# Band attention and two layers, one core: token tiles reused in place, first forms from sums made on GpSimd

## The chip, the cores and the metric

The program runs on one core of a Trainium2 chip in a single launch; the host only lays the arrays out. The metric is the device time of one execution in microseconds, from the first to the last instruction and what lies around them.

## The reference

Attention over 4 batches, 8 heads, 512 local and 32 global tokens, head dimension 64, and then two feed-forward layers on the 2176 tokens with model width 512 and inner width 2048. All in fp32:

```python
s_g = scale * q_g @ k_all.T ;  out_g = sm(s_g) @ v_all          # 32 global rows, all keys
s_ll = where(|pos_i - pos_j| <= 32, scale * q_l @ k_l.T, -1e9)  # band of the local rows
out_l = sm([scale * q_l @ k_g.T, s_ll]) @ [v_g, v_l]
x = [out_g, out_l], heads side by side                           # (2176, 512)
h = x @ w_in1 ;  x = where(h > 0, h, exp(min(h, 0)) - 1) @ w_out1
h = x @ w_in2 ;  x = where(h >= 1, h, where(h <= -1, 0, (h+1)**2/4)) @ w_out2
```

## The kernel before

**Arithmetic.** Each fp32 operand of a large product is split in two fp32r parts, high and low, and a product takes three matmuls (low by high, high by low, high by high). Weights come from DRAM as fp32 words which `decode` (L194) splits with integer operations on VectorE and copies on ScalarE; for up blocks `decode_in` (L872) also makes sums of blocks on GpSimd.

**Attention (L414 to L830).** 24 units, their instructions in a fixed order on each engine (`Pinned`). Meanwhile `prep` (L186) loads and decodes the weights of the inner blocks f = 0, 1, 2 of the first layer in six pieces through one tile `wraw`, and the first five up products are made. Each batch j leaves its 512 local tokens in `xh[j]`, `xl[j]`, 128x(4x512) in fp32r.

**Plain blocks.** For f = 0, 1, 2 (`PLAIN[0]`) and then f = 3 (`PLAIN[1]`) the first layer is computed directly: `plain` (up, L273), activation, `down` (L360), for each batch j. Down sums of f = 0, 1, 2 are evicted to DRAM (`collect`, L342); those of later blocks are accumulated there (L344). The 128 global tokens go as rows (L285, L373).

**Forms.** From f = 4 on, and in the whole second layer, two inner blocks and two batches (a duo: batches 0 and 1, or 2 and 3) are multiplied with 7 block products in place of 8 (`quad`, L1044). Each takes a form of the tokens (`X11, X21, X22`, which are quarters of the tokens as they are, and `T1` to `T4`, which are differences) of 128x1024 in two parts, 1 MB, and a form of the weights. 14 pairs of blocks, two duos each, make the groups (L1222). Only one duo's forms are in SBUF; the 28 forms lie in DRAM, and as the last product of a group is done with a form, that of the next group is loaded into its slot (`load_form`, L999).

**The first forms.** `keep_tokens` (L919) stores the tokens of each batch to `sums[0, j]`, high parts by SP (L922) and low parts by an accumulating DMA on GpSimd's queue (L923), and the halves that are `X11, X21, X22` as forms (L927). `first_forms` (L938) reads the sums back into one `wraw` tile, one `top` and one `rest` tile, takes four differences on VectorE, and makes T2, T3, T1, T4 one by one: `split` (ScalarE L934, VectorE L845) into a `wraw` tile and a store (L959). There are two `wraw` buffers and one of `top` and of `rest`. `decode_one` (f = 3), `decode_in`, `decode_out` and `first_forms` all pass through these three, and `in_order` (L171) keeps them in the order of the program on their tiles.

**Order.** After the attention a planner arranges instructions on each engine by a simulated timeline, within data dependences. The order of the program comes from `event` (L1170): at each event a product is issued, perhaps one `down`, and a step of the jobs that have come due (`job_at`). Jobs before: `decode_one` at 0, `decode_in(0)` at 2, `first_forms(0)` at 4, `decode_in(1)` at 8, `first_forms(1)` at 10, `decode_out(0)` at 13 and `decode_out(1)` at 14. The forms of the first group are loaded at event 13, after the token tiles have been closed (L1213).

Of the kernel before, what the change touches and what calls it, by code (L numbers as in the profile page):

```python
# [77 lines left out]
def band_attention_then_two_mlps(  # L78
# [32 lines left out]
    w_ctx, x_ctx = ExitStack(), ExitStack()  # L111
    ring_p = w_ctx.enter_context(tc.tile_pool(name="w", bufs=1))
    plain_p = x_ctx.enter_context(tc.tile_pool(name="xp", bufs=1))
    xh, xl = {}, {}
    for j in range(B):
        xh[j], xl[j] = (plain_p.tile([P, KT, SL], F32R, name=f"x{nm}{j}") for nm in "hl")
# [77 lines left out]
    def decode(wtmp_p, raw, hi, lo):  # L194

        n = raw.shape[1]
        words = raw.bitcast(U32).rearrange("p (n two) -> p n two", two=2)
        low, high = words[:, :, 0], words[:, :, 1]
        top = wtmp_p.tile([P, n], U32, tag="top", name="top")
        rest = wtmp_p.tile([P, n], U32, tag="rest", name="rest")  # L200
        yield

        if eng is free:
            in_order("top", eng.scalar.activation(top.bitcast(F32), high.bitcast(F32), AF.Abs))  # L204
        in_order(
            "rest",
            eng.vector.tensor_scalar(
                rest, high, 0x1FF, 15, ALU.bitwise_and, ALU.logical_shift_left
            ),
        )  # L210
# [12 lines left out]
        eng.vector.tensor_scalar(top, top, 3, 0x3FFFF000, ALU.logical_shift_left, ALU.bitwise_and)  # L223
        eng.vector.scalar_tensor_tensor(  # L224
            top, high, 0xC0000000, top, ALU.bitwise_and, ALU.bitwise_or
        )
        yield
        eng.scalar.activation(hi, top.bitcast(F32), AF.Copy)
        power = raw.bitcast(U32)[:, 0:n]
        eng.vector.tensor_scalar(power, top, 0xFF800000, None, ALU.bitwise_and)  # L230
        eng.vector.scalar_tensor_tensor(  # L231
            lo, rest, 2.0 ** -35, power.bitcast(F32), ALU.mult, ALU.mult
        )
# [24 lines left out]
    class Up:  # L258
# [8 lines left out]
        def products(self, m):  # L267
            ws = w_in[self.layer, self.f]
            for k in range(self.k, self.k + m):
                kt = k // 3  # L270
                w, x = ((ws[1], xh), (ws[0], xl), (ws[0], xh))[k % 3]
                w, x = w[:, kt * P:(kt + 1) * P], x[self.j][:, kt, :]
                eng.tensor.matmul(self.ps, w, x, start=k == 0, stop=k == 3 * KT - 1)  # L273
            self.k += m

# [122 lines left out]

    def x_high(j, kts, at, src):

        eng.scalar.activation(xh[j][:, kts[0]:kts[-1] + 1, at], src, AF.Copy)

    def x_low(j, kts, at, src):

        at = (slice(None), slice(kts[0], kts[-1] + 1), at)
        eng.vector.tensor_tensor(xl[j][at], src, xh[j][at].bitcast(F32), ALU.subtract)
# [493 lines left out]
    def decode_out(n):  # L900

        layer, fs = of_pair(n)
        i = (n + 1) % 3
        raw = words(DM, [(w1, w2)[layer][f][:, KT * P:] for f in fs])
        yield

        while w_out_uses.get(n - 3):
            yield
        w = w_ps[i].tile([P, 2, 2, DM], F32R, tag=f"wo{i}", name="wo")
        for _ in decode(wtmp_p, raw, *(w[:, i].rearrange("p f d -> p (f d)") for i in range(2))):  # L910
            pass
        for i, f in enumerate(fs):
            w_out[layer, f] = [w[:, part, i] for part in range(2)]

    def halves_of(t):

        return t.rearrange("p (k n) -> p k n", k=2)

    def keep_tokens():  # L919

        for j in range(B):
            eng.sync.dma_start(sums[0, j], xh[j].bitcast(F32))  # L922
            eng.gpsimd.dma_start(sums[0, j], xl[j].bitcast(F32), accum_op=ALU.add)  # L923
        for duo in range(2):
            for i, j, h in ((X11, 0, 0), (X21, 0, 1), (X22, 1, 1)):
                for part, x in enumerate((xh, xl)):
                    eng.sync.dma_start(  # L927
                        halves_of(forms[0, duo, i][:, part, :]),
                        x[2 * duo + j][:, 2 * h:2 * h + 2, :].bitcast(F32),
                    )  # L930

    def split(out, src):

        ins = eng.scalar.activation(out[:, 0], src, AF.Copy)  # L934
        add(out[:, 1], src, out[:, 0].bitcast(F32), ALU.subtract)
        return ins

    def first_forms(duo):  # L938

        s = wraw_p.tile([P, KT, SL], F32, tag="wraw", name="sum")
        in_order("wraw", eng.sync.dma_start(s, sums[0, 2 * duo]))
        parts = []
        for tag, h in (("top", 0), ("rest", 1)):
            t = wtmp_p.tile([P, 2 * SL], F32, tag=tag, name="half")
            in_order(tag, eng.sync.dma_start(halves_of(t), sums[0, 2 * duo + 1][:, 2 * h:2 * h + 2, :]))
            parts.append(t)
        yield
        x11, x21 = (s[:, 2 * h:2 * h + 2, :].rearrange("p k n -> p (k n)") for h in range(2))  # L950
        x12, x22 = parts
        add(x11, x12, x11, ALU.subtract)
        add(x12, x22, x12, ALU.subtract)
        add(x22, x22, x11, ALU.subtract)
        add(x21, x21, x22, ALU.subtract)
        for i, src in ((T2, x22), (T3, x12), (T1, x11), (T4, x21)):
            t = wraw_p.tile([P, 2, 2 * SL], F32R, tag="wraw", name="form")
            in_order("wraw", split(t, src))
            eng.sync.dma_start(forms[0, duo, i], t.bitcast(F32))  # L959
            made_forms.add((0, duo, i))  # L960
            yield

    def later_forms(duo):

        j0, j1 = 2 * duo, 2 * duo + 1

        def make(i, src):
            slot[i] = xs_p.tile([P, 2, 2 * SL], F32R, tag=f"x{i}", name="xs")
            split(slot[i], src)
            eng.sync.dma_start(forms[1, duo, i], slot[i].bitcast(F32))  # L970
            made_forms.add((1, duo, i))
            holds[i] = 1, duo

        def until(i):
# [23 lines left out]

    def load_form(layer, duo, i):  # L999

        slot[i] = xs_p.tile([P, 2, 2 * SL], F32R, tag=f"x{i}", name="xs")
        eng.sync.dma_start(slot[i].bitcast(F32), forms[layer, duo, i])
        holds[i] = layer, duo


# [17 lines left out]
    def product(n, duo, col, i, then):  # L1023
# [3 lines left out]
        for k in range(2):  # L1027
            for t, (a, b) in enumerate(((1, 0), (0, 1), (0, 0))):
                eng.tensor.matmul(  # L1029
                    ps,  # L1030
                    w[:, a, col + k * P:col + (k + 1) * P],
                    x[:, b, k * SL:(k + 1) * SL],
                    start=k + t == 0,
                    stop=k == 1 and t == 2,
                )
# [134 lines left out]
    def event(fn):  # L1170
# [7 lines left out]
        for job in line[:2]:  # L1178

            if job in line and (job is line[0] or (job[2] and not job[1])):  # L1180
                step(job)
        now[0] += 1

    def job_at(n, job, ahead=True):

        due.setdefault(n, []).append((job, ahead))

    keep_tokens()
# [5 lines left out]
    for duo in range(2):  # L1194
        made_forms.update((0, duo, i) for i in (X11, X21, X22))
    for i, fs in enumerate(PLAIN):
        for j in range(B):
# [5 lines left out]
        for j in range(B):  # L1203
            for f in fs:
                if (0, f, j) not in born:
                    if i:
                        need(lambda: (0, f) in w_in)
                    event(lambda: plain(0, f, j))
        event(begin)
    while downs and downs[0][2 if downs[0][0] == "down" else 4] == PLAIN[0]:  # L1210
        pop()
    need(lambda: all((0, duo, i) in made_forms for duo in range(2) for i in range(7)))
    x_ctx.close()  # L1213
    w_ctx.close()
    w_ps.append(mpool("w_third", 1))
    xs_p = mpool("xs", 1)
    w_ps.append(mpool("w_last", 1))
# [7 lines left out]
    job_at(base, decode_out(0))  # L1225
    for c in range(7):
        at = base + 17 * c
        job_at(at + 1, decode_out(2 * c + 1))
# [99 lines left out]
```

## Time and profile before

| | |
|---|---|
| time, median of 3 runs | 923.75 us (920.61 to 924.33) |
| profiled execution | 921.4 us, its span 919.6 us |
| busy in the span | PE 91%, VectorE 74%, ScalarE 60%, GpSimd 25% |
| mean granted TensorE clock | 0.957 |
| DMA | 196.59 MB, mean 214 GB/s |

PE is TensorE's matmuls, PEld its weight loads, DVE VectorE, ACT ScalarE, POOL GpSimd, SP SyncE; a q behind a name is the engine's queue (waits and DMA issues). `xs<-form` names an output and an input. In the views a wait `A <- B: us, times, longest` is idle time of A that B ended.

### The profile page before, as it was taken

How to read it: one execution, taken by the hardware profiler on the slowest of the kernel's cores; microseconds unless marked ns; L12 is line 12 of the kernel's file. 1: busy time of each engine (PE TensorE's matmuls, PEld its weight loads, DVE VectorE, ACT ScalarE, POOL GpSimd, SP SyncE). 2: the span in 40 equal slices, each digit the busy share in tenths (PEclk: the TensorE clock that was granted, in tenths of full speed). 3: DMA queues.
4: the chain of work that ended last, by engine and by line, in shares of the span. 5: the costliest groups of instructions: out<-in, count | busy, mean ns of one | idle time of the engine just before them, and what ended most of it. 6: DMA issues, size and time to landing. Idle time of an engine off the chain costs nothing.

```text
span 919.6 us, 15850 instructions
## 1 busy us (share of the span) xinstructions
PE 832.7 (91%) x6058; PEld 673.3 (73%) x6058; DVE 684.8 (74%) x1187; ACT 556.0 (60%) x948; POOL 227.3 (25%) x250
## 2 busy tenths in 40 slices
PE   8769779999942699999999998899989999999998
PEld 5647557887721588888888887688778888888886
DVE  5758567745441999998597988979998889876563
ACT  5657566655451556665563645777787677667461
POOL 2121210402240055345141003033053244421000
PEclk9999899999975799999999999899999999999999
DMA  8997995749999474996495294644676197519733
GB/s 263 326 329 264 298 314 190 231 190 361 362 228 299 166 129 113 294 254 126 69 296 185 98 369 174 256 155 140 208 260 145 26 292 256 94 38 283 258 108 103
DMA packets 59788, 196.59 MB, mean 214 GB/s; under 512 B 8513, under 2 KB 8769, under 8 KB 48193
## 3 DMA queue, kind: packets, MB, share of 16 engines
q1 hardware_dynamic: 47328, 170.15, 51.7%
q0 software_dynamic: 12096, 25.17, 16.9%
q8 instruction: 48, 0.79, 0.3%
q10 hardware_dynamic: 288, 0.26, 0.1%
q14 instruction: 28, 0.22, 0.1%
HBM read 123.99 MB, written 71.57 MB: 213 GB/s over the span
## 4 chain that ended last, share of the span: by engine, by line
PE 62%; DVE 14%; DMA 13%; ACT 5%; issue 3%; POOL 2%; SPq 0%; DVEq 0%; ACTq 0%; POOLq 0%
PE dn L360 28%; PE up L1029 21%; DMA wraw<-in_w 7%; DMA form<-form 3%; PE up L273 2%; DMA half<-sum 2%; DVE u L845 2%; DVE rest L211 2%; PE dn L373 2%; PE s L141 2%; POOL mixed L845 1%; DVE top L224 1%; PE up L285 1%; PE up L141 1%; ACT sn L141 1%
## 5 line engine op out<-in xcount | busy, mean ns | idle before, releaser
L1029 PE MATMUL up<-xs,wi 128*128 128x512 f32 x1176 | 296.0, 398 | 23.8 <-DMA xs<-form 17.1
L360 PE MATMUL dn<-gh,wo 128*128 128x512 f32 x928 | 288.0, 396 | 17.1 <-DVE wo L231 11.2
L1029 PEld LDWEIGHTS up<-xs,wi 128*128 128x128 f32 x1176 | 223.8, 192 | 75.8 <-DMA xs<-form 10.6
L360 PEld LDWEIGHTS dn<-gh,wo 128*128 128x128 f32 x928 | 175.1, 191 | 58.0 <-DVE wo L231 12.5
L360 PE MATMUL dn<-gl,wo 128*128 128x512 f32 x464 | 178.2, 394 | 1.4 <-DVE gl L326 1.4
L845 DVE TENSOR_TENSOR u<-up,u 128x512 f32<-128x512 f32 x196 | 130.6, 684 | 42.4 <-PE up L1029 39.3
L344 POOL DMA_DIRECT2D sum<-ev x80 | 73.2, 1144 | 202.5 <-ACT ev L339 201.7
L322 ACT ACTIVATE gh<-g 128x512 fp32r<-128x512 f32 x123 | 77.5, 630 | 72.1 <-DVE g L305 33.6
L326 DVE TENSOR_TENSOR gl<-g,gh 128x512 fp32r<-128x512 f32 x123 | 102.7, 842 | 23.5 <-ACT gh L322 22.4
L360 PEld LDWEIGHTS dn<-gl,wo 128*128 128x128 f32 x464 | 88.3, 190 | 20.5 <-DVE gl L326 1.8
L845 POOL TENSOR_TENSOR whole<-wi 128x1024 f32<-128x1024 f32 x14 | 36.7, 2624 | 259.6 <-DVE wi L231 183.6
L298 ACT ACTIVATE g<-u,half_sb 128x512 f32<-128x512 f32 x64 | 45.8, 720 | 51.6 <-DVE u L845 44.2
L307 DVE TENSOR_TENSOR g<-u,g 128x512 f32<-128x512 f32 x64 | 52.0, 815 | 25.7 <-ACT g L300 25.6
L339 ACT ACTIVATE ev<-dn 128x512 f32<-128x512 f32 x110 | 60.6, 595 | 10.8 <-DMA sum<-ev 5.4
L293 ACT ACTIVATE g<-u 128x512 f32<-128x512 f32 x48 | 30.2, 629 | 52.4 <-DVE u L845 48.5
L305 DVE SCALAR_TENSOR_TENSOR g<-u,g 128x512 f32<-128x512 f32 x48 | 40.3, 842 | 18.7 <-ACT g L295 18.7
L211 DVE SCALAR_TENSOR_TENSOR rest<-wraw,rest 128x1024 uint32<-128x1024 uint32 x29 | 53.2, 1834 | 0.2
L299 ACT ACTIVATE g<-g,one_sb 128x512 f32<-128x512 f32 x68 | 48.6, 719 | 1.3
L295 ACT ACTIVATE g<-g,one_sb 128x512 f32<-128x512 f32 (+1 forms) x64 | 45.7, 716 | 1.6
L204 ACT ACTIVATE top<-wraw 128x1024 f32<-128x1024 f32 x29 | 33.3, 1147 | 19.4 <-DMA wraw<-in_w 15.8
L141 POOL TENSOR_SCALAR k_sb<-k_sb 128x512 f32<-128x512 f32 (+1 forms) x46 | 21.6, 486 | 89.2 <-DMA k_sb<-in_kT 64.0
L300 ACT ACTIVATE g<-g 128x512 f32<-128x512 f32 x68 | 42.3, 626 | 1.2
(172 smaller groups left out, 1197.2 us busy)
## 6 DMA issues: line engine op xcount, KB each, us to landing
xs<-form SPq DMA_DIRECT2D x49, 1024.0 KB, 9.3
wraw<-in_w SPq DMA_DIRECT2D x56, 512.0 KB, 6.5
sum<-ev POOLq DMA_DIRECT2D x80, 256.0 KB, 8.3
v_sb<-in_vwin SPq DMA_DIRECT2D x64, 260.0 KB, 5.3
form<-xs SPq DMA_DIRECT2D x14, 1024.0 KB, 4.1
sum<-ev SPq DMA_DIRECT2D x32, 256.0 KB, 3.1
sum<-sum SPq DMA_DIRECT2D x8, 1024.0 KB, 4.9
form<-form SPq DMA_DIRECT2D x8, 1024.0 KB, 5.6
```

The source lines that it names most:

```text
L141: return lambda *args, **kw: tc.keep_in_program_order(fn(*args, **kw))
L211: eng.vector.scalar_tensor_tensor(rest, low, 17, rest, ALU.logical_shift_right, ALU.bitwise_or)
L298: eng.scalar.activation(self.g, self.ps, AF.Relu, bias=half_sb, scale=-0.5)
L299: eng.scalar.activation(self.g, self.g, AF.Relu, bias=one_sb, scale=-1.0)
L307: eng.vector.tensor_tensor(g, self.ps, g, ALU.max)
L322: eng.scalar.activation(self.gh, self.g, AF.Copy)
L326: eng.vector.tensor_tensor(self.gl, self.g, self.gh.bitcast(F32), ALU.subtract)
L339: eng.scalar.activation(out, ps, AF.Copy)
L344: eng.gpsimd.dma_start(to, out, accum_op=ALU.add)
L360: eng.tensor.matmul(banks[d], w[:, d * P:(d + 1) * P], g, start=first and k == 0, stop=last and k == 2)
L845: return (engine or eng.vector).tensor_tensor(out, a, b, op)
L1029: eng.tensor.matmul(ps, w[:, a, col + k * P:col + (k + 1) * P], x[:, b, k * SL:(k + 1) * SL], start=k + t == 0, stop=k == 1 and t == 2,)
```

## The change

- The token tiles become 16 tiles of 128x(2x512) (a half of the model width, one part, one batch), in a pool that lives to the end. `PLACES` gives each of the 7 forms one of these places; X11, X21 and X22 of the first duo are the tokens where they lie. The eighth place takes every third block of decoded down weights. The pool `xs`, and `w_last`, are gone.
- `keep_tokens` is gone. `first_forms` adds high and low parts on GpSimd, straight from the token tiles, into the tiles that held the sums before. The copies of X11, X21, X22 to DRAM wait for the last low part of the attention (`last_low`) and are issued by `first_forms`; there is no accumulating DMA of tokens.
- Jobs: `first_forms(0)` at 0, `first_forms(1)` at 2, `decode_one` at 4, `decode_in(0)` at 7, `decode_out(0)` at 9, `decode_in(1)` at 11. With more than two jobs in line an event takes two rounds of steps. f = 3 takes the batches in the order 2, 3, 0, 1, and the early weights' memory is given up after its first batch.
- In the attention's `decode` the last step uses a tile `power` of its own instead of writing over `wraw`.

```diff
-    plain_p = x_ctx.enter_context(tc.tile_pool(name="xp", bufs=1))
+    plain_p = ctx.enter_context(tc.tile_pool(name="xp", bufs=1, reuse_waits="tile"))
+    def token_tile(j, h, part):
+        return plain_p.tile([P, 2, SL], F32R, tag=f"x{part}{j}{h}", name="x" + "hl"[part])
...
+        if eng is pinned:
+            power = wtmp_p.tile([P, n], U32, tag="power", name="power")
+        else:
+            power = raw.bitcast(U32)[:, 0:n]
...
-        power = raw.bitcast(U32)[:, 0:n]
         eng.vector.tensor_scalar(power, top, 0xFF800000, None, ALU.bitwise_and)
...
+        last_low[0] = eng.vector.tensor_tensor(out, src, high, ALU.subtract)
...
+        while len(w_ps) < 2:
+            yield
+        if i < 2:
+            w = w_ps[i].tile([P, 2, 2, DM], F32R, tag=f"wo{i}", name="wo")
+            w = [w[:, part] for part in range(2)]
+        else:
+            w = [token_tile(1, 0, part) for part in range(2)]
...
-    def keep_tokens():
-        for j in range(B):
-            eng.sync.dma_start(sums[0, j], xh[j].bitcast(F32))
-            eng.gpsimd.dma_start(sums[0, j], xl[j].bitcast(F32), accum_op=ALU.add)
...
+    PLACES = {X11: (0, 0), X21: (0, 1), X22: (1, 1), T2: (2, 0), T3: (2, 1), T1: (3, 0), T4: (3, 1)}
+    def new_form(i):
+        slot[i] = [flat(token_tile(*PLACES[i], part)) for part in range(2)]
+        return slot[i]
...
+    def keep(form, key, after=None):
+        for part in range(2):
+            ins = eng.sync.dma_start(forms[key][:, part], form[part].bitcast(F32))
+            if after is not None:
+                tc.add_manual_dep(ins.ins, after.ins.name, LANDED, reason="behind the loads")
+        made_forms.add(key)
...
     def first_forms(duo):
-        s = wraw_p.tile([P, KT, SL], F32, tag="wraw", name="sum")
-        in_order("wraw", eng.sync.dma_start(s, sums[0, 2 * duo]))
...
+        s = wraw_p.tile([P, 2, 2 * SL], F32, tag="wraw", name="sum")
+        x11, x21 = s[:, 0], s[:, 1]
+        x12, x22 = (wtmp_p.tile([P, 2 * SL], F32, tag=tag, name="half") for tag in ("top", "rest"))
+        for out, j, h, tag in ((x11, j0, 0, "wraw"), (x12, j1, 0, "top"), (x22, j1, 1, "rest"), (x21, j0, 1, "")):
+            high, low = (flat(x[j][h]).bitcast(F32) for x in (xh, xl))
+            ins = add(out, high, low, engine=eng.gpsimd)
+            if tag:
+                in_order(tag, ins)
+        for i, j, h in ((X11, j0, 0), (X21, j0, 1), (X22, j1, 1)):
+            keep([flat(x[j][h]) for x in (xh, xl)], (0, duo, i), last_low[0])
         yield
         add(x11, x12, x11, ALU.subtract)
         ...
         for i, src in ((T2, x22), (T3, x12), (T1, x11), (T4, x21)):
             t = wraw_p.tile([P, 2, 2 * SL], F32R, tag="wraw", name="form")
+            t = [t[:, part] for part in range(2)]
             in_order("wraw", split(t, src))
-            eng.sync.dma_start(forms[0, duo, i], t.bitcast(F32))
-            yield
+            keep(t, (0, duo, i))
+            if i == T3:
+                yield
...
-    job_at(0, decode_one(PLAIN[1][0]))
-    job_at(2, decode_in(0))
-    job_at(4, first_forms(0), False)
-    job_at(8, decode_in(1))
-    job_at(10, first_forms(1), False)
+    job_at(0, first_forms(0), False)
+    job_at(2, first_forms(1), False)
+    job_at(4, decode_one(PLAIN[1][0]))
+    job_at(7, decode_in(0))
+    job_at(9, decode_out(0))
+    job_at(11, decode_in(1))
+    for i, js in enumerate(((0, 1, 2, 3), (2, 3, 0, 1))):
...
-    for i in range(7):
+    for i, (j, h) in ((X11, (0, 0)), (X21, (0, 1)), (X22, (1, 1))):
+        slot[i] = [flat(x[j][h]) for x in (xh, xl)]
+        holds[i] = 0, 0
...
+    for i in (T2, T3, T1, T4):
         load_form(0, 0, i)
```

## Rows read from the trace of the kernel before

**Rows 1.** The page: busy tenths of TensorE, 40 slices of 23 us

```profile
PE   8769779999942699999999998899989999999998
```

**Rows 2.** Engine times by stage: busy us (instructions), clock, DMA share, GB/s

```profile
0.00:150.00 150.00, 118.52 (x2846) 88.55 (x2850) 96.20 (x441) 93.86 (x244) 30.91 (x85) 0.94 0.88 291
155.30:219.40 64.10, 64.10 (x296) 53.56 (x294) 39.25 (x48) 40.37 (x63) 9.22 (x7) 1.00 0.71 242
219.40:252.00 32.60, 29.23 (x131) 23.45 (x131) 18.27 (x27) 14.94 (x24) 12.70 (x11) 0.95 1.04 381
252.00:312.20 60.20, 21.94 (x60) 14.68 (x58) 27.51 (x31) 21.61 (x31) 9.55 (x11) 0.60 0.88 252
```

**Rows 3.** Waits, 160 to 320 us: us in total, times, longest

```profile
PE up L1029 <- DMA xs<-form: 17.1, 3, 9.8
PE dn L360 <- DVE wo L231: 11.2, 2, 10.3
```

**Rows 4.** The chain that ended last, 150 to 420 us: start, us, what

```profile
206.23 1.24 DVE form L845
...
216.18 1.17 ACT top L204
...
230.75 2.38 POOL wi L845
...
233.15 19.61 DMA half<-sum
...
260.18 6.11 DMA form<-form
...
268.74 10.51 DMA form<-form
...
288.46 1.24 DVE form L845
...
290.56 8.61 DMA wraw<-in_w
...
299.26 0.71 DVE rest L207
...
304.57 1.24 DVE wo L231
```

**Rows 5.** Timeline of SP's queue: first stores of the made forms

```profile
186.58 6.54 SPq L959 DMA_DIRECT2D form<-form  x2
```

**Rows 6.** Instructions of L923: count, ns min/median/max, first and last start

```profile
L923 POOL DMA_DIRECT2D sum<-xl x4: 878/884/1024, 52.2 to 161.8; - x4
```

**Rows 7.** Timeline of VectorE in the attention: two stretches

```profile
26.17 0.43 DVE L141 TENSOR_SCALAR rest<-wraw 128x512 uint32<-128x512 uint32 x1 [2.88 <-DMA wraw<-in_w]
...
87.51 0.69 DVE L141 SCALAR_TENSOR_TENSOR top<-wraw,top 128x512 uint32<-128x512 uint32 x1
...
91.64 0.69 DVE L141 SCALAR_TENSOR_TENSOR wl<-rest,wraw 128x512 fp32r<-128x512 uint32 x1
```

**Rows 8.** Waits of SP's queue, 0 to 150, and of VectorE, 0 to 160

```profile
SPq L141 <- DVE wl L141: 12.7, 4, 4.3
...
DVE rest L141 <- DMA wraw<-in_w: 18.9, 6, 5.4
```

**Rows 9.** Groups of TensorE instructions by line, 155.3 to 330 us

```profile
L360 PE MATMUL dn<-gh,wl 128*128 128x512 f32 x42 | 16.4, 392 | 0.0
L273 PE MATMUL up<-xh,wl 128*128 128x512 f32 x24 | 9.3, 389 | 0.0
```

**Rows 10.** Timeline of all engines, 223.3 to 228.3 us

```profile
223.38 2.40 POOL L845 TENSOR_TENSOR whole<-wi 128x1024 f32<-128x1024 f32 x1 [48.00 <-DVE wi L231]
...
227.04 1.14 DVE L326 TENSOR_TENSOR gl<-g,gh 128x512 fp32r<-128x512 f32 x1 [0.70 <-ACT gh L322]
...
228.10 0.68 DVE L845 TENSOR_TENSOR u<-up,u 128x512 f32<-128x512 f32 x1
```

**Rows 11.** Timeline of ScalarE: first write of the new top tile

```profile
151.04 1.17 ACT L204 ACTIVATE top<-wraw 128x1024 f32<-128x1024 f32 x1 [0.67 <-PE po L141]
```

More of the change, by code (lines that the diff above doesn't have):

```diff
@@ L110, in band_attention_then_two_mlps @@
     ev_p = [ctx.enter_context(tc.tile_pool(name="ev", bufs=2))]
-    w_ctx, x_ctx = ExitStack(), ExitStack()
+    plain_p = ctx.enter_context(tc.tile_pool(name="xp", bufs=1, reuse_waits="tile"))
+    w_ctx = ExitStack()
     ring_p = w_ctx.enter_context(tc.tile_pool(name="w", bufs=1))
-    plain_p = x_ctx.enter_context(tc.tile_pool(name="xp", bufs=1))
+    def token_tile(j, h, part):
+        return plain_p.tile([P, 2, SL], F32R, tag=f"x{part}{j}{h}", name="x" + "hl"[part])
     xh, xl = {}, {}
     for j in range(B):
-        xh[j], xl[j] = (plain_p.tile([P, KT, SL], F32R, name=f"x{nm}{j}") for nm in "hl")
+        for part, x in enumerate((xh, xl)):
+            x[j] = [token_tile(j, h, part) for h in range(2)]
     xh[GR], xl[GR] = (xpool.tile([P, KT, B * SG], F32R, name=f"x{nm}{GR}") for nm in "hl")
@@ L271, in products @@
                 w, x = ((ws[1], xh), (ws[0], xl), (ws[0], xh))[k % 3]
-                w, x = w[:, kt * P:(kt + 1) * P], x[self.j][:, kt, :]
+                w, x = w[:, kt * P:(kt + 1) * P], x[self.j][kt // 2][:, kt % 2, :]
                 eng.tensor.matmul(self.ps, w, x, start=k == 0, stop=k == 3 * KT - 1)
@@ L399, in x_high, with tokens @@
     def x_high(j, kts, at, src):
-        eng.scalar.activation(xh[j][:, kts[0]:kts[-1] + 1, at], src, AF.Copy)
+        eng.scalar.activation(tokens(xh, j, kts, at), src, AF.Copy)
     def x_low(j, kts, at, src):
-        at = (slice(None), slice(kts[0], kts[-1] + 1), at)
-        eng.vector.tensor_tensor(xl[j][at], src, xh[j][at].bitcast(F32), ALU.subtract)
+        out, high = tokens(xl, j, kts, at), tokens(xh, j, kts, at).bitcast(F32)
+        last_low[0] = eng.vector.tensor_tensor(out, src, high, ALU.subtract)
+    def tokens(x, j, kts, at):
+        if j == GR:
+            return x[j][:, kts[0]:kts[-1] + 1, at]
+        return x[j][kts[0] // 2][:, kts[0] % 2:kts[-1] % 2 + 1, at]
+    last_low = [None]
     def mpool(name, bufs, **kw):
@@ L908, in decode_out @@
             yield
-        w = w_ps[i].tile([P, 2, 2, DM], F32R, tag=f"wo{i}", name="wo")
-        for _ in decode(wtmp_p, raw, *(w[:, i].rearrange("p f d -> p (f d)") for i in range(2))):
+        while len(w_ps) < 2:
[5 more added lines that the diff above has]
+            w = [token_tile(1, 0, part) for part in range(2)]
+        for _ in decode(wtmp_p, raw, *(part.rearrange("p f d -> p (f d)") for part in w)):
@@ L911, in decode_out @@
             pass
         for i, f in enumerate(fs):
-            w_out[layer, f] = [w[:, part, i] for part in range(2)]
-    def halves_of(t):
-        return t.rearrange("p (k n) -> p k n", k=2)
-    def keep_tokens():
-        for j in range(B):
-            eng.sync.dma_start(sums[0, j], xh[j].bitcast(F32))
-            eng.gpsimd.dma_start(sums[0, j], xl[j].bitcast(F32), accum_op=ALU.add)
[L924 to L930, printed above, removed]
+            w_out[layer, f] = [part[:, i] for part in w]
@@ L932, in split, with flat @@
+    PLACES = {X11: (0, 0), X21: (0, 1), X22: (1, 1), T2: (2, 0), T3: (2, 1), T1: (3, 0), T4: (3, 1)}
+    def flat(t):
+        return t.rearrange("p k n -> p (k n)")
+    def new_form(i):
+        slot[i] = [flat(token_tile(*PLACES[i], part)) for part in range(2)]
+        return slot[i]
     def split(out, src):
-        ins = eng.scalar.activation(out[:, 0], src, AF.Copy)
-        add(out[:, 1], src, out[:, 0].bitcast(F32), ALU.subtract)
-        return ins
-    def first_forms(duo):
-        s = wraw_p.tile([P, KT, SL], F32, tag="wraw", name="sum")
-        in_order("wraw", eng.sync.dma_start(s, sums[0, 2 * duo]))
[L944 to L948, printed above, removed]
+        ins = eng.scalar.activation(out[0], src, AF.Copy)
+        add(out[1], src, out[0].bitcast(F32), ALU.subtract)
+        return ins
@@ new lines, in keep @@
+    def keep(form, key, after=None):
[4 more added lines that the diff above has]
+        made_forms.add(key)
+    def first_forms(duo):
+        j0, j1 = 2 * duo, 2 * duo + 1
+        s = wraw_p.tile([P, 2, 2 * SL], F32, tag="wraw", name="sum")
[8 more added lines that the diff above has]
+            keep([flat(x[j][h]) for x in (xh, xl)], (0, duo, i), last_low[0])
@@ L949, in first_forms @@
         yield
-        x11, x21 = (s[:, 2 * h:2 * h + 2, :].rearrange("p k n -> p (k n)") for h in range(2))
-        x12, x22 = parts
         add(x11, x12, x11, ALU.subtract)
@@ L957, in first_forms @@
             t = wraw_p.tile([P, 2, 2 * SL], F32R, tag="wraw", name="form")
+            t = [t[:, part] for part in range(2)]
             in_order("wraw", split(t, src))
-            eng.sync.dma_start(forms[0, duo, i], t.bitcast(F32))
-            made_forms.add((0, duo, i))
-            yield
+            keep(t, (0, duo, i))
+            if i == T3:
+                yield
     def later_forms(duo):
@@ L967, in make @@
         def make(i, src):
[L968 to L971, printed above, removed]
+            split(new_form(i), src)
+            keep(slot[i], (1, duo, i))
             holds[i] = 1, duo
@@ L999, in load_form @@
     def load_form(layer, duo, i):
-        slot[i] = xs_p.tile([P, 2, 2 * SL], F32R, tag=f"x{i}", name="xs")
-        eng.sync.dma_start(slot[i].bitcast(F32), forms[layer, duo, i])
+        for part, t in enumerate(new_form(i)):
+            eng.sync.dma_start(t.bitcast(F32), forms[layer, duo, i][:, part])
         holds[i] = layer, duo
@@ L1031, in product @@
                     w[:, a, col + k * P:col + (k + 1) * P],
-                    x[:, b, k * SL:(k + 1) * SL],
+                    x[b][:, k * SL:(k + 1) * SL],
                     start=k + t == 0,
@@ L1177, in event @@
         line.extend([job, 0, ahead] for job, ahead in due.pop(now[0], []))
-        for job in line[:2]:
-            if job in line and (job is line[0] or (job[2] and not job[1])):
-                step(job)
+        for _ in range(2 if len(line) > 2 else 1):
+            for job in line[:2]:
+                if job in line and (job is line[0] or (job[2] and not job[1])):
+                    step(job)
         now[0] += 1
@@ L1186, in job_at @@
         due.setdefault(n, []).append((job, ahead))
-    keep_tokens()
-    job_at(0, decode_one(PLAIN[1][0]))
-    job_at(2, decode_in(0))
-    job_at(4, first_forms(0), False)
-    job_at(8, decode_in(1))
-    job_at(10, first_forms(1), False)
[L1194 to L1197, printed above, removed]
+    job_at(0, first_forms(0), False)
[5 more added lines that the diff above has]
+    for i, js in enumerate(((0, 1, 2, 3), (2, 3, 0, 1))):
+        fs = PLAIN[i]
+        for j in js:
             for f in fs:
@@ L1202, in band_attention_then_two_mlps @@
         downs.append(item)
-        for j in range(B):
+        for j in js:
             for f in fs:
@@ L1208, in band_attention_then_two_mlps @@
                     event(lambda: plain(0, f, j))
+            if len(w_ps) < 2 and i:
+                while downs[0][2 if downs[0][0] == "down" else 4] == PLAIN[0]:
+                    pop()
+                w_ctx.close()
+                w_ps.append(mpool("w_third", 1))
         event(begin)
-    while downs and downs[0][2 if downs[0][0] == "down" else 4] == PLAIN[0]:
-        pop()
+    for i, (j, h) in ((X11, (0, 0)), (X21, (0, 1)), (X22, (1, 1))):
+        slot[i] = [flat(x[j][h]) for x in (xh, xl)]
+        holds[i] = 0, 0
     need(lambda: all((0, duo, i) in made_forms for duo in range(2) for i in range(7)))
[L1213 to L1217, printed above, removed]
-    for i in range(7):
+    for i in (T2, T3, T1, T4):
         load_form(0, 0, i)
```

1 line of the change is left out of this document (removed).

## The prediction

> **What bounds the kernel now.** I read the page's slices first, then a table of engine times by stage, then the waits and the chain inside the stages that stood out.
>
> In the slices TensorE is full almost everywhere [rows 1]; it is short in the first seven (the attention) and in slices 12 to 14, from 253 to 322 us. By stage [rows 2]: PE is busy 118.5 of the first 150 us, with the DMA engines at a share of 0.88; all of 155.3 to 219.4; 29.2 of 32.6 us to 252; and 21.9 of 60.2 us to 312.2, at a mean granted clock of 0.60. The full stage makes 296 matmuls in 64.1 us, 0.2166 us each. At that pace the 131 + 60 = 191 matmuls of 219.4 to 312.2 need 41.4 of 92.8 us: **51.4 us are lost there**.
>
> What PE waits for there is loads of forms (17.1 us) and decoded weights (11.2 us) [rows 3]. The chain tells why [rows 4]: one string of jobs goes through two `wraw` buffers and single `top` and `rest` tiles, one after another. The second duo's first forms wait 19.61 us for token sums read back from DRAM; its four made forms then go out one at a time, because one `wraw` buffer holds the sum till the last form and all four use the other. T2's split ends at 260.18, T4's at 289.70: 29.5 us for three cycles of store and split, 9.8 each, a store taking up to 10.51. For the first duo the cycles start at 186.58 [rows 5] and end at 207.47: 7.0 each, a store down to 3.88. Only at 290 does the next weight load start, and PE resumes when it is decoded.
>
> **The change, part by part.** A is 155.3 us, where the attention leaves PE.
>
> *Attention.* Three of four batches of token copies leave it (the four accumulating stores start from 52.2 to 161.8 [rows 6], the fourth batch after A): by the code 3 MB of high parts, 3 MB accumulated, and about 5 of 6 MB of form halves, 11 of the 43.7 MB that 291 GB/s moves in 150 us. The raw weights come free after `top` (ends 88.20 in one round) instead of after `wl` (92.33) [rows 7]: the next load can be issued 4.1 us sooner, and SP has 12.7 us of waits for `wl` with value loads queued behind [rows 8]. VectorE waits 18.9 us in six places for raw weights [rows 8]; the first, 2.88 us at 26.17 [rows 7], is older than any copy or reuse and stays, so at most 16.0 us can go. PE has 31.5 idle us there, so they can come through, but what is late next (the unit's own PE, ScalarE and VectorE chain) keeps some. I take 12, nearer the upper end as both edits act on the same wait; bounds 0 and 16.
>
> *Order of jobs.* Both duos' forms now come before the decode of the fourth plain block (f = 3), in the same single-file string. PE's work without that block is, after A, 72 up matmuls, 126 down matmuls (each row of [rows 9] stands for three alike), and 12 + 9 for the rows: 219, at 0.2166 us 47.4 us. So PE runs dry at A+47.4. When is f = 3 ready?
> - Sums, duo 0: a GpSimd add of 128x1024 takes 2.40 us [rows 10], in place of the DRAM round trip. `top` is first written at 151.04 before [rows 11], A-4.3; the two sums that need `top` and `rest` end at about A+0.5, the VectorE differences (1.24 each, as the split's subtraction of the same shape [rows 4]) at A+3, T2's split (1.06 + 1.24, beside the end of the attention) at A+8.
> - T2's store queues behind the held copies: 12 of 512 KB, 6.3 MB, released by the last low part near A+2. At the 381 GB/s of [rows 2] that is 16.5 us, and T2 its own 2.8: landed at A+22, T3 split at A+24.4, T4 two cycles of 7.0 later, A+38.4.
> - Duo 1: its sum needs the buffer that T4 frees: add 2.4, differences and split 7.7: A+48.5. Three cycles of 7.5 (near the 7.0, PE's own stores beside them): A+71.
> - f = 3: a load of 1 MB, 2.8 us at 381 GB/s and 8.61 under load [rows 2, 4]; I take 6; decode 6.5 (299.26 to 305.81 [rows 4]): A+83.5.
>
> PE stands 83.5 - 47.4 = **36 us**. Bounds: 19.1 and 53.5, from the rivals below.
>
> *Behind it.* An up decode takes 17.0 us (216.18 to 233.13 [rows 4]), an out decode 6.5: pair 0 at A+100.5, its out part A+107, pair 1 A+124. PE has f = 3's 111 matmuls (24.0 us), pair 0's 42 and one down of 12 (11.7): dry at A+119.2. **4.8 us**, bounds 0 and 10. The old stall of 51.4 us goes whole: its causes are behind.
>
> *Clock.* From 252 the clock was mostly at the lower of its two levels (1.2 of 2.4 GHz) and 60 matmuls took 21.9 us instead of 13.0 [rows 2]: 8.9 us, part of the 51.4. After one long stall instead of many short ones I take 3 (0 to 8.9).
>
> *Adds beside VectorE.* One VectorE subtraction from SBUF took 1.14 us beside a GpSimd add, where the neighbouring one took 0.68 [rows 10]: 0.46 more. Eight adds: 3.7 us, of which I count 2 on the path (0 to 3.7). The Trainium skill, "SBUF — State Buffer", section "Who interferes with whom", says more: a VectorE instruction with two SBUF inputs and a GpSimd instruction that reads SBUF exclude each other, and the later blocks until the first is done. The rows agree in direction, with 0.46 in place of 2.40. By the rule the four adds at the attention's end would cost up to 9.6 us rather than 2, and the sum would be 8 higher.
>
> *At nothing:* three of the seven forms are no longer loaded (3 MB, which lay beside f = 3's work), form loads in halves, and the tile place for every third out block. From 320 on the work is the same; a different order there may give or take 5 us.
>
> Sum, against the profiled execution (span 919.6, whole 921.4): 921.4 - 51.4 - 12 + 36 + 4.8 + 3 + 2 = 903.8. The median is 2.35 above that execution, so 906.
>
> **Rivals.**
> 1. *Slower: the form string holds f = 3 too long.* Cycles as the second duo had them: T2 landed at A+22, T3 split 24.4, T4 44; duo 1's three adds in queue order and split +12.4, 56.4; three cycles of 9.8, 85.8; load 8.61 and decode 6.5, A+101. Stall 53.5. It decides from there: 51.4 + 12 - 9.8 = 53.6 of stall eats everything. If the attention then gives only 5 and the adds cost 3.7: 930, as a median 932. For: every form of duo 1 took this long. Against: that was beside form loads and accumulations, which now come later.
> 2. *Faster: the copies do not hold T2.* Stores of 3.88, cycles 6.3: T4 of duo 0 at A+27, T4 of duo 1 at A+54, f = 3, with the load of 6, at A+66.5: stall 19.1. With 16 from the attention and 1 for the adds, clock 0: 878.9, median 881. For: SP may queue T2 before duo 1's copies. Against: 6.3 MB must go out somewhere in that time.
> 3. *The attention gives nothing:* another wait ends last in each unit. 915.8, median 918. For: ScalarE is busy 94 of 150 us and PE 118.5; against: the six waits stand on VectorE, whose order is fixed, so nothing behind them can pass.
> 4. *GpSimd's lock as the page has it:* 911.8, median 914.
>
> **How the numbers follow.** A measurement of this kernel tells about 0.5%, 4.6 us, from no change. Forecast (896 to 914): 0.40. Rival 2 and its neighbourhood (under 896): 0.20. Rivals 3 and 4 (914 to 919): 0.14. Rival 1: 0.26, of which 0.12 within 0.5% and 0.14 slower. So faster 0.74, same 0.12, slower 0.14. The range leaves a tenth at either end: 882 to 930.
>
> **What would show it.** Right: VectorE's waits for raw weights under 5 us in all in the attention, its end near 143; GpSimd adds of 2.4 us at its end, no read of sums; made forms with a store between each two; one PE stall of some 36 us behind the plain blocks ending with the decode of f = 3, a short one before pair 1, then PE full. Wrong: an attention that ends near 155 (rival 3); the f = 3 decode over 100 us behind the attention (rival 1) or within 70 (rival 2); f = 3 decoded ahead of duo 1's forms, by which the order of the string would be misread.

## The result, and the profile after

The changed kernel takes **890.96 us** in the median (890.76 to 895.01, 4 runs) against 923.69 us of the kernel before beside it: a ratio of **0.9662** (95% interval 0.9628 to 0.9697), 3.4% faster. The forecast was 906 us with a range of 882 to 930. The profiled execution is 890.8 us, its span 889.0 us.

The page's slices of TensorE, 22.2 us each, answer to [rows 1]: of the first six, the second, third, fifth and sixth are fuller, and the hole has moved to the ninth, from 178 to 200 us.

```profile
PE   7899999906969999999999996999989999999998
```

By stage, as [rows 2] (span of the stage, busy us of PE, PEld, DVE, ACT, POOL with their instructions, clock, DMA share, GB/s): the attention up to its first down product, the plain blocks without f = 3, the stall, and what follows.

```profile
0.00:123.84 123.84, 109.21 (x2894) 83.00 (x2894) 95.43 (x442) 93.44 (x245) 33.26 (x84) 1.00 0.75 243
128.30:176.20 47.90, 47.90 (x217) 39.61 (x215) 30.13 (x29) 26.95 (x43) 10.38 (x5) 1.00 0.76 291
176.20:207.00 30.80, 0.24 (x2) 0.24 (x2) 11.02 (x12) 7.34 (x8) 0.00 (x0) 0.54 0.63 230
207.00:228.00 21.00, 21.00 (x87) 17.28 (x88) 17.38 (x21) 13.27 (x22) 9.95 (x9) 0.86 0.90 312
228.00:260.00 32.00, 23.35 (x91) 17.24 (x90) 14.60 (x21) 13.63 (x23) 15.50 (x18) 0.95 1.05 231
260.00:300.00 40.00, 38.43 (x171) 30.37 (x170) 32.84 (x43) 24.12 (x38) 15.22 (x13) 0.96 0.80 228
```

The same 2894 TensorE instructions up to the first down product took 150.90 us before, with PE busy 119.42 us at a mean clock of 0.94 and DMA engines at 0.88:

```profile
0.00:150.90 150.90, 119.42 (x2894) 89.31 (x2894) 96.42 (x442) 94.23 (x245) 30.91 (x85) 0.94 0.88 290
```

Now they take 123.84 us, busy 109.21 at 1.00. The attention leaves TensorE at 128.3 us instead of 155.3: **27.0 of the 30.6 us** by which the span is shorter. All that follows takes 760.7 us instead of 764.3.

VectorE's waits for raw words in the attention, 18.9 us in [rows 8], are one:

```profile
DVE rest L146 <- DMA wraw<-in_w: 2.6, 1, 2.6
```

The waits behind the attention (of A for B: us, times, longest) answer to [rows 3]. The loads of forms and the out decode are gone from the list; f = 3 is on it, and evictions that wait for the stores of earlier ones.

```profile
PE up L281 <- DVE wo L239: 30.6, 1, 30.6
ACT ev L347 <- DMA sum<-ev: 23.7, 12, 5.1
...
PE dn L368 <- ACT ev L347: 4.9, 4, 3.0
...
PE dn L381 <- ACT ev L347: 3.6, 1, 3.6
```

The chain of the same stretch (start, us, what), as [rows 4]: made forms go out one at a time as before, but each store on the chain takes 2.6 to 4.3 us, and no read of sums is left. At 205.48 begins the last operation that f = 3 waits for; from 227.71 the chain runs over accumulating stores.

```profile
160.98 2.63 DMA form<-form
...
176.95 4.32 DMA form<-form
...
183.68 2.64 DMA form<-form
...
188.76 2.63 DMA form<-form
...
194.26 5.89 DMA wraw<-in_w
...
205.48 1.24 DVE wo L239
...
227.71 5.93 DMA sum<-ev
```

### The profile page after: what moved, and what is told of

It is laid out like the page before. It is cut to its first block, busy times and chain, and to the rows that moved or that the text cites. A ratio compares the mean times of both kernels' runs of the same rounds, so it can differ in the third digit from the quotient of the medians.

```text
span 889.0 us, 15955 instructions
## 1 busy us (share of the span) xinstructions
PE 818.1 (92%) x6058; PEld 663.3 (75%) x6058; DVE 687.3 (77%) x1187; ACT 553.0 (62%) x948; POOL 247.3 (28%) x254
## 4 chain that ended last, share of the span: by engine, by line
PE 54%; DVE 20%; issue 7%; ACT 6%; DMA 6%; POOL 6%; SPq 0%; ACTq 0%; POOLq 0%; DVEq 0%
PE dn L368 24%; PE up L1053 18%; DVE u L861 3%; DVE gl L334 2%; DVE g L315 2%; DMA sum<-ev 2%; PE up L281 2%; POOL mixed L861 2%; DVE rest L220 2%; POOL whole L861 2%; PE s L146 2%; PE dn L381 2%; DVE top L233 1%; POOL sum L352 1%; DMA wraw<-in_w 1%
## 5 line engine op out<-in xcount | busy, mean ns | idle before, releaser
L1053 PE MATMUL up<-xh,wi 128*128 128x512 f32 x784 | 263.2, 395 | 8.9 <-DVE u L861 6.0
L368 PE MATMUL dn<-gh,wo 128*128 128x512 f32 x608 | 189.3, 394 | 8.6 <-ACT ev L347 5.2
L1053 PEld LDWEIGHTS up<-xh,wi 128*128 128x128 f32 x784 | 148.7, 190 | 44.2 <-DVE u L861 9.4
L1053 PE MATMUL up<-xl,wi 128*128 128x512 f32 x392 | 154.2, 393 | 0.0
L368 PEld LDWEIGHTS dn<-gh,wo 128*128 128x128 f32 x608 | 113.1, 189 | 35.9 <-ACT ev L347 9.3
L368 PE MATMUL dn<-gl,wo 128*128 128x512 f32 x304 | 116.8, 391 | 0.3 <-DVE gl L334 0.3
L1053 PEld LDWEIGHTS up<-xl,wi 128*128 128x128 f32 x392 | 74.5, 190 | 15.1
L368 PE MATMUL dn<-gh,xl 128*128 128x512 f32 x160 | 62.5, 393 | 0.5 <-DVE xl L239 0.4
L368 PE MATMUL dn<-gh,xh 128*128 128x512 f32 x160 | 62.3, 390 | 0.0
L368 PE MATMUL dn<-gl,xh 128*128 128x512 f32 x160 | 59.2, 389 | 0.0
L307 ACT ACTIVATE g<-g,one_sb 128x512 f32<-128x512 f32 x68 | 48.6, 719 | 1.3
```

Of the source, the lines that this page charges most:

```text
L307: eng.scalar.activation(self.g, self.g, AF.Relu, bias=one_sb, scale=-1.0)
L368: eng.tensor.matmul(banks[d], w[:, d * P:(d + 1) * P], g, start=first and k == 0, stop=last and k == 2)
L1053: eng.tensor.matmul(ps, w[:, a, col + k * P:col + (k + 1) * P], x[b][:, k * SL:(k + 1) * SL], start=k + t == 0, stop=k == 1 and t == 2,)
```

## The experiments

First the end of the attention. The table has the start of the first down product (in us) and TensorE in the stage up to it; raw early is the change's own tile for the last decode step. The last two columns are TensorE's waits in that stage: for `o_sb`, which VectorE makes from the attention's output and which stands behind the decode in its fixed order, and those before the products `s` and `po`, which read keys and values, for which the profile shows no releaser (`issue`).

| kernel | raw words | token traffic in the attention | down starts | PE busy | clock | `o_sb` | `s`, `po` |
|---|---|---|---|---|---|---|---|
| before | late | halves and sums, 11 MB | 150.9 | 119.4 | 0.94 | 9.7 | 14.0 |
| b1_raw_early | early | halves and sums, 11 MB | 147.7 | 121.0 | 0.92 | 8.4 | 11.1 |
| b2_copies_held | late | none | 139.1 | 115.4 | 0.94 | 16.8 | 1.0 |
| a1_raw_late | late | none | 136.5 | 113.6 | 0.95 | 15.4 | 2.0 |
| after | early | none | 123.8 | 109.2 | 1.00 | 0.9 | 8.2 |
| a2_copies_early | early | halves, 5 MB | 127.9 | 111.0 | 1.00 | 3.1 | 6.4 |
| c2_added_sums | early | halves and sums, low parts added | 142.4 | 118.3 | 0.95 | 4.4 | 11.2 |
| c1_plain_sums | early | halves and sums, plain stores | 143.3 | 118.4 | 0.96 | 3.1 | 14.0 |

The six runs below whose edits leave the attention as it is in the changed kernel (a3, a5, a6, a8, a9, a10) start the down product at 122.7 to 127.0 us. So a few us between two single traces show nothing.

**a1_raw_late.** The changed kernel, one edit undone:

```diff
-        if eng is pinned:
-            power = wtmp_p.tile([P, n], U32, tag="power", name="power")
-        else:
-            power = raw.bitcast(U32)[:, 0:n]
+        power = raw.bitcast(U32)[:, 0:n]
```

Expected: 

> The changed kernel with one edit undone: in the attention the last step of a decode writes over the raw words again, so that a raw tile comes free only after the low part. The measure is the end of the attention on TensorE (128.3 us in the changed kernel, 155.3 before). Theory (the held copies made the attention short, the early release little): it ends near 131, the whole time 3 us longer, about 894. Rival (the early release made most of it): it ends near 140, the waits of VectorE for raw words come back to some 12 us, time about 903.

Measured: 904.55 us, ratio 0.9794 (0.9759 to 0.9829); down at 136.5, 12.7 us later. The rival is nearer. VectorE's waits for raw words come back, 17.2 of the 18.9 us, though the share of the DMA engines in the stage is 0.67 instead of 0.88:

```profile
DVE rest L146 <- DMA wraw<-in_w: 17.2, 6, 3.7
```

**a2_copies_early.** The changed kernel with `keep(..., (0, duo, i))`, without `last_low[0]`.

Expected: 

> The changed kernel with the copies of X11, X21, X22 not held behind the last low part, so that they may go out during the attention (5 of their 6 MB; there are still no sums in DRAM). Theory (DMA traffic made the attention long): it ends near 140, VectorE waits for raw words some 6 us, the granted clock dips below 1.00 in some stretch, time about 900, less what the forms gain from a queue free of copies (up to 6 us). Rival (the early release made most of it): it ends within 3 us of 128.3 and the time is 885 to 892.

Measured: 887.63 us, 0.9623 (0.9580 to 0.9666), which the intervals do not tell from the changed kernel. The down starts 4.1 us later, at the edge of that spread, so 5 MB of halves are not what made the attention long. The stall before f = 3 is shorter by 9.5 us than the 30.56 of the changed kernel, since of the twelve copies SP issues only two ahead of T2's store and none behind it (in a8 below none lie there at all, and the stall is the same):

```profile
201.31 0.79 PE L281 MATMUL up<-xh,wo 128*128 128x512 f32 x1 [21.09 <-DVE wo L239]
```

So holding the copies back wins 4 us at most and costs some 9: the hold is not where the gain comes from.

**b2_copies_held.** The kernel before; each of its token copies gets the wait:

```diff
+        def held(ins):
+            tc.add_manual_dep(ins.ins, last_low[0].ins.name, LANDED, reason="behind the loads")
-            eng.sync.dma_start(sums[0, j], xh[j].bitcast(F32))
+            held(eng.sync.dma_start(sums[0, j], xh[j].bitcast(F32)))
```

Expected: 

> The kernel before with one edit: the token copies and the form halves wait for the last low part of the attention; raw words are still released late and sums still go through DRAM. Theory (DMA traffic): the attention ends near 133 instead of 155.3, its mean clock near 1.00. Rival (early release): it ends at 145 or later with VectorE's waits for raw words over 10 us. In both, the forms come later, because sums are read back only after 14 MB of copies; the whole time is 905 to 925.

Measured: 953.26 us, slower: 1.0321 (1.0284 to 1.0359), beyond what either theory gave. The down starts at 139.1, 11.8 us earlier than before; the waits for raw words stay:

```profile
DVE rest L141 <- DMA wraw<-in_w: 17.8, 6, 3.4
```

The time is lost behind it, where sums can be read only after all copies:

```profile
PE up L1034 <- DMA xs<-form: 23.5, 2, 18.7
PE dn L360 <- ACT ev L339: 19.6, 8, 6.7
...
PE up L1034 <- DVE wi L231: 10.9, 1, 10.9
```

**b1_raw_early.** The kernel before with the edit that a1 undoes.

Expected: 

> The kernel before with one edit: in the attention the last step of a decode uses a tile of its own, so raw words come free earlier; the token copies go out during the attention as before. The start of the down products after the attention stood at 150.9 us before, 123.8 in the changed kernel, 139.1 with the copies held alone. Theory now (two separate costs, 12 to 13 us each): it starts near 138, the clock 1.00 most of the time. Rival (either edit alone would do, once the raw words come early the copies hide): it starts at 131 or sooner. Time 925 less that, plus or minus 4.

Measured: 918.56 us, 0.9936 (0.9915 to 0.9958), 4.9 us under the kernel before beside it; down at 147.7. Neither theory: the early release alone moves the down by 3.2 us, with waits of 13.9 us left.

```profile
DVE rest L141 <- DMA wraw<-in_w: 13.9, 4, 5.2
```

The two edits are not two separate costs (3.2 + 11.8 = 15.0, together 27.1). A raw load must be issued and must land. Released late, it comes about 3 us short (six waits of 2.9 us in the mean in a1) at a DMA share of 0.67 over the stage; released early, it still comes short while the DMA engines are full (0.90 in b1). Only both together take the wait away, and only then does the clock stay at its upper level. The last columns of the table part the two: waits for `o_sb` are long, 15.4 and 16.8 us, where raw words come late and no sums are stored, and the waits before `s` and `po` are long, 11.1 to 14.0 us, in every kernel that stores the sums, early or late. That the latter are late key and value loads is likely, but the profile names no releaser. The two edits were not made together on the kernel before: pairs that agree in both edits as far as the attention goes, b1 and c2, b2 and a1, lie 5.3 and 2.6 us apart, so a few of the 27.1 us may be due to that rest.

**c2_added_sums and c1_plain_sums.** Which traffic? On a2, the sums of the kernel before are put back, never read: as they were (c2), or with both parts as plain stores on SP's queue (c1):

```diff
+            eng.sync.dma_start(sums[0, j][:, 2 * h:2 * h + 2, :], xh[j][h].bitcast(F32))
+            eng.gpsimd.dma_start(sums[0, j][:, 2 * h:2 * h + 2, :], xl[j][h].bitcast(F32), accum_op=ALU.add)   # c2
+            eng.sync.dma_start(other[j][:, 2 * h:2 * h + 2, :], xl[j][h].bitcast(F32))                         # c1
```

Expected of c2: 

> The changed kernel with the form halves copied during the attention (the down products then started at 127.9 us) and, besides, the sums of the kernel before put back: high parts stored by SP, low parts added in DRAM by GpSimd's queue, never read. Theory (with raw words released early it is the sums, 6 of the 11 MB, that lengthened the attention to 147.7): the down products start at 144 to 150. Rival (the old place of the stores and tiles made it): under 135.

Expected of c1: 

> As c2, but high and low parts both go out as plain stores on SP's queue to places of their own: the same 8 MB leave SBUF, nothing is added in DRAM and GpSimd's queue waits for nothing. Theory (the adding store is what costs: it must read DRAM, and GpSimd's key copies wait in line behind it): the down products start at 129 to 134. Rival (bytes of the stores cost, of whichever kind): 140 or later.

Measured, in 2 runs each: 902.91 us with the down at 142.4, a little under its 144 to 150, and 902.32 us with the down at 143.3, the rival. The adding store is not dearer here than the plain one; it is the stores themselves that cost, by their bytes or their number, which was not separated. The stretch from 25 to 125 us in c1, and then in a2: the DMA engines full against 0.81, and the clock below 1.00.

```profile
25.00:125.00 100.00, 80.17 (x2047) 60.93 (x2047) 71.87 (x308) 66.17 (x171) 20.17 (x55) 0.96 0.98 342
```

```profile
25.00:125.00 100.00, 86.94 (x2265) 67.28 (x2246) 80.51 (x353) 75.23 (x197) 26.93 (x62) 1.00 0.81 279
```

So the sums, some 6 MB in the attention that the change makes needless, cost 14.5 to 15.4 us there; the 4.1 of the halves is within what single traces differ by.

Then what follows the attention.

**a3_f3_first.** The changed kernel with `decode_one` at event 0 and the first forms at 2 and 4.

Expected: 

> The changed kernel with the decode of block f = 3 at event 0 and the first forms at events 2 and 4. Theory (the jobs are one string through two raw buffers and single tiles, so its length decides and not its order): TensorE runs on for 24 us longer, then stands until pair 0 is decoded; the idle time of TensorE behind the plain blocks is the same within 8 us (the decode can start a little before the attention ends), time 884 to 892. Rival (only the place of f = 3 makes the stall): the 30.6 us stall goes with no new one over 10 us, time under 872.

Measured: 892.06 us, 0.9659 (0.9625 to 0.9694), as the changed kernel. The 30.6 us wait is gone and these, 31.2 us, stand in its place. The time is what the theory gave, but only 13.9 us of them are for the decode of pairs 0 and 1, as it had it; 17.3 are for evictions, beside full DMA engines (1.04 to 1.08 from 200 to 230 us). That the length of the string decides fits this and a6 below, and is not shown by a3 alone.

```profile
PE dn L381 <- ACT ev L347: 11.1, 1, 11.1
...
PE up L1053 <- DVE wi L239: 8.9, 2, 5.8
...
PE dn L368 <- ACT ev L347: 6.2, 5, 3.0
...
PE up L1053 <- POOL wi L861: 5.0, 2, 4.7
```

**a5_f3_plain_store.** The condition in `collect` becomes `if 0 in fs or 3 in fs:`; the additions of f = 3 to what f = 0, 1, 2 left are missing.

Expected: 

> The changed kernel; the down sums of f = 3 are written by plain stores on SP's queue over those of f = 0, 1, 2 instead of being added to them in DRAM by GpSimd's queue (the sum then lacks those blocks). Theory (the 12 us that TensorE loses from 228 to 260 us are evictions waiting for accumulating stores): the waits of ScalarE for stored evictions fall from 23.7 to under 8 us, time 881 to 886. Rival (those waits lie beside the wait for pair 1's decode, which ends last): time 888 to 892.

Measured: 885.45 us, 0.9583 (0.9549 to 0.9617), some 5.5 us under the changed kernel, as the theory had it, though the waits fall to 8.8 us and not under 8. Waits of ScalarE from 207 to 300 us, the changed kernel and then this one:

```profile
ACT ev L347 <- DMA sum<-ev: 21.1, 11, 5.1
```

```profile
ACT ev L347 <- DMA sum<-ev: 8.8, 4, 5.3
```

**a6_side_tiles.** T2 and T1 through `wraw` as before, T3 and T4 beside it:

```diff
+            if i in (T3, T4):
+                for k in range(2):
+                    cut = slice(k * SL, (k + 1) * SL)
+                    t = [u_p.tile([P, SL], F32R, tag="u", name="side") for part in range(2)]
+                    split(t, src[:, cut])
+                    for part in range(2):
+                        eng.sync.dma_start(forms[0, duo, i][:, part, cut], t[part].bitcast(F32))
```

Expected: 

> The changed kernel; T3 and T4 are split in halves into four small tiles each (the tiles that the block products use later), so that only T2 and T1 go through the raw buffer, and a split need not wait for the store ahead of it. Theory (a store between each two splits makes the string long): the eight forms take some 15 us less, the TensorE stall before f = 3 falls from 30.6 to 12 to 18 us, time 875 to 884. Rival (splits wait for ScalarE and VectorE, or for the sums, not for stores): stall over 26, time 888 to 892.

Measured: **873.5 us**, 0.9455 (0.9424 to 0.9486), a little better than expected; the stall is inside the forecast. The one free raw buffer did make the string long.

```profile
195.72 0.79 PE L281 MATMUL up<-xh,wo 128*128 128x512 f32 x1 [16.37 <-DVE wo L239]
```

**a8_copies_last.** The copies are issued in `decode_one` behind its load: `keep(..., (0, duo, i), last_load[0])`.

Expected: 

> The changed kernel; the twelve copies of X11, X21, X22 wait for the raw words of f = 3 instead of the last low part of the attention, so they are clear of the attention and of the stores of the made forms. Theory (held copies slow the made forms' stores: the stall was 21.1 us with copies early, 30.6 with copies held): the attention stays at 123.8, stall 20 to 23, time 880 to 884. Rival (the copies then sit ahead of the loads of pair 0 and give it back): stall before f = 3 of 20 to 23, but a new wait of 8 us or more for the decode of pair 0, time 887 to 892.

Measured: 880.62 us (874.98 to 883.67), 0.9523 (0.9471 to 0.9575). The theory holds: the stall is as with copies early, and the attention keeps its length (down at 123.3):

```profile
196.67 0.79 PE L281 MATMUL up<-xh,wo 128*128 128x512 f32 x1 [21.04 <-DVE wo L239]
```

**a9_both** has both edits, **a10_both_f3_first** besides the order of a3.

Expected of a9: 

> The changed kernel with the two edits that helped: T3 and T4 through small tiles (873.5 us alone), and the copies behind the raw words of f = 3 (880.6 alone). Theory (one shortens the string, the other clears its stores): the stall before f = 3 falls from 16.4 and 21.0 to 5 to 12 us, time 862 to 870. Rival (behind side tiles the held copies no longer matter, and behind f = 3 they sit before the loads of the first group): 871 to 876.

Expected of a10: 

> As a9 with the decode of f = 3 ahead of the first forms. Theory (one string, its length decides): within 4 us of a9, the stall before f = 3 gone and one before pair 0 in its place. Rival (evictions of f = 3 come earlier, beside no others, and the copies go out 40 us earlier into the stores of the forms): 5 us or more off either way.

Measured: a9 875.37 us, 0.9481 (0.9440 to 0.9522), no better than a6, as its rival said. Its stall is down to 7.0 us, but now TensorE waits for the first group's forms, whose loads SP issues from 199.8 us, behind the twelve copies (180.4 to 193.2). That the copies make them late was not tested by itself:

```profile
PE up L281 <- DVE wo L239: 7.0, 1, 7.0
...
PE up L1064 <- DMA xh<-form: 6.8, 2, 3.8
...
PE up L1064 <- DMA xl<-form: 3.8, 2, 2.0
```

a10 takes **862.59 us**, 0.9352 (0.9319 to 0.9384), 12.8 us under a9 where I expected 4 at most: the rival. It beats both kernels; these are the longest of its TensorE waits behind the attention:

```profile
PE dn L368 <- ACT ev L347: 9.4, 9, 3.8
...
PE up L1064 <- DVE u L862: 2.3, 3, 1.4
PE dn L381 <- ACT ev L347: 2.1, 1, 2.1
```

With the short string the order matters, as it did not in a3: the 24 us of f = 3 now cover the forms, and no wait for form loads is left in the list. The copies and the evictions of f = 3 also go out earlier, as the rival named; what each of these gives was not separated.

## Why the prediction was right, and where it was not

The sign, and the place of the gains, were right; the size was about half (17.6 us of span forecast, 30.6 measured), and one term, the attention, makes the miss. The other terms missed too and offset each other, which is luck.

- **Attention, forecast 12 (0 to 16), measured 27.0.** This step failed in its size. The waits for raw words went as bounded, 18.9 to 2.6, so 16.3 us. But I took the waits of one engine as the bound of the stage. TensorE's idle time fell by 16.9 us (31.5 to 14.6). That this is near the 16.3 is in part chance: its waits for `o_sb`, behind VectorE, fell by 8.8 us, those before `s` and `po`, in which VectorE has no part by the profile, by 5.8. And its busy time fell by 10.2 us for the same instructions; no term stood for that. Some of it is the clock: before, it was at its lower level (0.50, which is 1.2 GHz) in four stretches, 17.1 us in all, with TensorE busy 15.0 of them. At the upper level that work would take half, so the clock is at most 7.5 of the 10.2 us (an estimate from these rows). The rest need not be longer matmuls: the 64 products `sg` of 128x416 take 516 ns each before and 514 after, yet keep TensorE busy for 10.2 and 7.6 us, so fewer of them overlapped. "Both edits act on the same wait" was half true: b1 and b2 show that either alone leaves it, b2 that the copies also cost 11.8 us apart from it. Through which loads those went is open. TensorE's waits of the two kinds, before and after:

```profile
PE ot L141 <- DVE o_sb L141: 9.7, 5, 3.9
PE po L141 <- issue: 7.0, 5, 2.0
PE s L141 <- issue: 7.0, 5, 2.8
```

```profile
PE ot L146 <- DVE o_sb L146: 0.9, 2, 0.5
PE po L146 <- issue: 4.7, 4, 1.6
PE s L146 <- issue: 3.5, 4, 1.6
```

- **The stall, forecast 36, measured 30.6.** TensorE ran dry 47.9 us after A (forecast 47.4), f = 3 was ready at 78.4 (forecast 83.5). T2's split ends at A+7.0 (8), T3's begins at 146.55, A+18.2 (T2 landed at A+22), duo 0's T4 is split at A+37.7 (38.4), duo 1's T2 at A+48.6 (48.5). The near agreement for duo 0 is luck: SP issued six of the twelve copies ahead of T2's store and six behind it, as rival 2 had thought possible, and T3's split ended at A+20.6 instead of 24.4; but the two cycles to T4 took 8.6 us each instead of 7.0. What made the stall shorter is duo 1's cycles, 5.6 instead of 7.5, while TensorE stood and SP issued no other stores (182.42 to 194.15 us). The two splits on ScalarE between which T2's store lies:

```profile
132.99 1.06 ACT L951 ACTIVATE form<-half 128x1024 fp32r<-128x1024 f32 x1 [0.16 <-DVE half L861]
...
146.55 1.06 ACT L951 ACTIVATE form<-half 128x1024 fp32r<-128x1024 f32 x1 [0.45 <-DMA form<-form]
```

- **Behind it, forecast 4.8, measured 15.3.** From 228 to 260 us 91 matmuls took 32.0 us, 12.3 more than at 0.2166 us each, and 3.0 were lost to 300. The decode of pair 1 is not among TensorE's waits there. Of its 10.2 idle us from 228 to 300, 8.5 ended with ScalarE's evictions; that these wait for accumulating stores of f = 3 a5 shows for 5.5 us of the whole. What made the rest is open. This wait was in none of my rivals.
- **Clock after the stall, forecast 3, measured 2.2** (87 matmuls in 21.0 us, 0.86).
- **GpSimd's adds, forecast 2, measured 2.2 on the string.** Here the rule of the Trainium skill ("SBUF — State Buffer", "Who interferes with whom") was right and my reading of [rows 10] too mild: the VectorE difference that starts during a GpSimd add ends 1.1 us after it, having taken 3.39 us; the next one takes 1.23. The 0.46 us of [rows 10] was only the end of such a wait: the add of 128x256 beside that subtraction was over 0.60 us after it began. The same is seen at 126.45 us with 3.40, and two low parts of 0.69 each take 3.49 together beside the add at 148.95. It is a full block, but only three of the eight adds met one. The one near 170 us lies on the string; the one at 126.45 lies ahead of T2's split of duo 0, whose store went out behind copies all the same. VectorE and GpSimd near 166 to 172 us:

```profile
166.12 4.74 POOL L861 TENSOR_TENSOR sum<-xh,xl 128x1024 f32<-128x1024 f32 x2 [14.39 <-DVE form L861]
...
168.55 3.39 DVE L861 TENSOR_TENSOR sum<-half,sum 128x1024 f32<-128x1024 f32 x1 [2.51 <-POOL sum L861]
```

```profile
171.98 1.23 DVE L861 TENSOR_TENSOR half<-half 128x1024 f32<-128x1024 f32 x1
```

- **The sum behind the attention** (lost time and its replacements): forecast 5.6 us gained, measured 3.6. The wholes agree because a shorter stall and a longer tail offset each other.

Of the rivals, the third (the attention gives nothing) is out; the second named a real price, copies ahead of T2: its stall of 19.1 us is near the 21.1 and 21.0 measured with the copies early or last, but the change as it is pays for them, six of them ahead of T2 and six between T2 and T3. The first, slower, did not come: f = 3 was ready 22.6 us before the point from which it decides (A+101). The fourth was right in kind, but of the four adds at the attention's end only one blocked an operation.

## What to carry to other kernels

A load that an in-order engine waits for has two ends, its release and its landing; while the queue is full or the release is late, mending one of them may give a fraction of what both give together, so test them as a pair. When a stage has many short waits on TensorE's path, count the clock too: here up to 7.5 of the 27.0 us won in the stage were the same matmuls at the higher clock. And where several jobs share one ring of buffers, their order may cost nothing while the ring's work is long (a3), and matter once it is short (a10).

## What the runs showed of the hardware

- Stores of 6 MB more in the attention cost as much plain (down at 143.3) as with half of them added in DRAM (142.4), against 127.9 without them.
- A VectorE subtraction with both inputs in SBUF does not slow down beside a GpSimd add, it waits for its end: 3.39 and 3.40 us instead of 1.23, ending 1.1 us after the add.
- TensorE's granted clock was 1.00 through the whole attention of the changed kernel and 0.94 on average before; the same 2894 instructions were busy 109.2 and 119.4 us, and at most 7.5 us of that difference is the clock (15.0 us of TensorE's work lay at the lower level).
